# A 64-byte shift of the attention stage's tiles in SBUF

## The chip, the cores and the metric

The kernel runs on one core of one Trainium2 chip. The metric is device time of one execution in microseconds (us). The chip's engines go by short names: PE is TensorE (its matmuls; PEld are its weight loads, LDWEIGHTS), DVE is VectorE, ACT is ScalarE, POOL is GpSimd, and SP is SyncE, which issues all DMAs of this kernel. SBUF is the on-chip memory of 128 partitions; an "address" below is a byte offset inside a partition, the same in all of them.

## The reference

The input `x` is 2048 rows of 1024 float32 values. A conditioning vector gives six modulation rows (`mod`). The computation is one transformer-like block:

```python
h = _layernorm(x) * (1 + ca) + sa
x = x + ga * _A_ref(h, wq, wk, wv, wo, beta)     # attention with a memory
h = _layernorm(x) * (1 + cb) + sb
x = x + gb * _B_ref(h, w1, b1, w2, b2)           # MLP across the tokens
```

`_A_ref` projects `h` to queries, keys and values of 32 heads of 32 values, and cuts the 2048 rows into four segments of 512. In each segment a head does causal softmax attention, reads a memory matrix M with phi(q), mixes the two by a gate, and adds phi(k) v of the segment to M. The result goes through `wo`. `_B_ref` multiplies with a 2048 x 3584 matrix along the tokens, applies GELU, and multiplies back.

## The kernel before

Every large float32 product is done in three matmuls of `float32r` operands: each operand is split into a high part and a rest ("hi" and "lo"), and the products (hi, hi), (hi, lo), (lo, hi) are added in PSUM. So one operand tile of 512 columns is a `[128, 2, 512]` tile: 2048 bytes of hi, then 2048 bytes of lo.

The attention stage fills the first 1020 us. The normed input `h` lies in 16 "pages" of the pool `page` (`new_page`), one for each of 8 blocks of 128 channels and two segments at a time. The weights of one group of four heads lie in tiles `w` of the pool `paw` (tag `w`, 8 of them): `wv` holds keys and values, `wq` the queries. There are 32 iterations: two passes over pairs of segments, in each pass eight groups, in each group two segments. An iteration projects in two ways, and these two lines are where `w` and the pages meet on PE:

- `kv_chunk` (line 185, PSUM tile `nps`): the page is the stationary operand, 128 columns, and `w` the moving one, 256 columns. 96 matmuls an iteration, 3072 in all.
- `q_chunk` (line 193, PSUM tile `qps`): `w` is the stationary operand, 128 columns, and the page the moving one, 512 columns. 24 an iteration, 768 in all.

Each matmul has a weight load of its own, which runs beside the matmul ahead of it.

Between the projections of one iteration PE does the attention of others: `maxima` (line 421, `sx`, `sy`, `sz`) and `scores` (lines 443 to 450, `a`) read both operands out of one stacked tile `sk`; `values` (line 471, `pv`) multiplies the probabilities `ph` with `vp`; `memory` (lines 393 and 403, `rd` and `up`) reads and updates M (`MZ`); lines 353 and 486 transpose keys and results with the unit matrix `ident`. The order of the work is the order in which the main loop calls these pieces (`scores`, then `maxima` three heads ahead, then `values` one behind, then a piece of `project` eight ahead), as a planner that estimates times has interleaved them; the engines' queues keep that order. SP loads `w` tiles from DRAM for later groups (`load_w`), the second half of the modulation (`rawm`, line 497), stored input (`hre`), and copies `sg` into `sk` (`stack`).

After the attention come the output projection (`out_proj`, line 649, `po`: the pages hold `wo`, the stationary operand is `ots`) up to about 1253 us, and the MLP (`mix`, line 741, `mx`: the stationary operand is `sp`, the moving one `bA`, `bB` or `bU`) to the end. Both have the same three-product order and 512 moving columns as `q_chunk`.

SBUF is handed out in the order in which pools are opened. On the left side lie `const`, `page`, `par`, then `acst`, and above it the attention's other pools: `paw`, `st1`, later `prj`, `late` and `sk0`, `sk1`. On the right side lie `top` and, below it, `st2` and later `late2`. `acst` begins with a tile that nothing reads or writes, `pad2`. The output projection and the MLP close the attention's pools and place their own tiles from `page` upward and from the right end downward.

Of the kernel before, what the change touches and what calls it, by code (L numbers as in the profile page):

```python
# [7 lines left out]
F32 = mybir.dt.float32  # L8
# [10 lines left out]
P = 128  # L19
# [25 lines left out]
def attention_and_mlp(ctx, tc, x, wq, wkv, wo, beta, w1, b1, w2, b2, c, wm_a, wm_b, out):  # L45
# [22 lines left out]
    acst = acst_pool.__enter__()  # L68
    top_pool = tc.tile_pool(name="top", bufs=1, side="right")
    top = top_pool.__enter__()  # L70
    top.tile([P, 8], F32, name="pad")
    acst.tile([P, 8], F32, name="pad2")
    psum = ctx.enter_context(tc.tile_pool(name="psum", bufs=1, space=PSUM))

    def bank(tag, bufs, name):
# [868 lines left out]
```

## Time and profile before

| | us |
|---|---|
| median of 3 runs before | 2337.69 (2335.87 to 2338.27) |
| the profiled execution's own time | 2335.59 |
| its span, first to last instruction | 2333.9 |
| PE busy with matmuls | 2243.0 |
| PE busy with weight loads | 1925.1 |
| DVE busy | 1725.1 |
| ACT busy | 1102.0 |
| POOL busy | 678.4 |

The profiled execution is one run; its time is 2.10 us under the median of the three timed runs. A row of a group of instructions gives their line, engine, operation, the tiles (output, then inputs), the shapes, the count, the busy time in us and the mean duration of one in ns. The busy time is the time in which at least one of them ran: since matmuls are pipelined, the durations overlap, and 389 ns for one matmul doesn't mean that one starts each 389 ns. In a run of equal matmuls the time from one start to the next ("the step") is (length of the run - duration of the last) / (count - 1).

### The profile page before, as it was taken

To read this page: it belongs to the slowest core of one execution; us is meant where nothing else is said; L and a number is where in the kernel's file an instruction comes from. 1 tells how busy PE (TensorE), PEld (TensorE's weight loads), DVE (VectorE), ACT (ScalarE), POOL (GpSimd) and SP (SyncE) were. 2 spreads that over 40 slices of the span, in tenths; PEclk is the share of its full clock that TensorE was granted. 3 is DMA by queue.
4 is the path that set the end of the run, shared out by engine and by line. 5 is a ranking of instruction groups with operands and counts; after the bars stand their busy time and mean duration, and the time that the engine had idled before them with its cause. 6 is when DMAs were issued, how large, how long until landed. Compare 5 with 4: busy or idle time off the path is not lost.

```text
span 2333.9 us, 38273 instructions
## 1 busy us (share of the span) xinstructions
PE 2243.0 (96%) x13866; PEld 1925.1 (82%) x13866; DVE 1725.1 (74%) x3838; ACT 1102.0 (47%) x2002; POOL 678.4 (29%) x683
## 2 busy tenths in 40 slices
PE   8989999988889999998999999999999999999999
PEld 7888888877789999986877888888888788888887
DVE  6677777677766656657988656598889787868687
ACT  5476776645556666654334333353335242424232
POOL 3154544567755555545000000023332000000000
PEclk9999999999999999998999999999999999999999
DMA  6856666578844444473454765365557542423234
GB/s 244 250 153 178 179 186 184 166 231 260 259 131 115 129 119 119 106 229 129 149 195 166 295 228 198 140 252 213 214 213 272 185 136 72 145 66 129 68 112 150
DMA packets 164272, 406.27 MB, mean 174 GB/s; under 512 B 17108, under 2 KB 63220, under 8 KB 155124
## 3 DMA queue, kind: packets, MB, share of 16 engines
q1 hardware_dynamic: 164084, 403.83, 53.4%
q8 instruction: 110, 1.80, 0.3%
q14 instruction: 78, 0.64, 0.1%
HBM read 232.04 MB, written 120.86 MB: 151 GB/s over the span
## 4 chain that ended last, share of the span: by engine, by line
PE 80%; DVE 9%; DMA 6%; issue 2%; ACT 2%; SPq 1%; POOL 0%; DVEq 0%; ACTq 0%
PE mx L741 42%; PE nps L185 12%; PE qps L193 7%; PE po L649 6%; PE pv L471 3%; DMA rawm<-in_wm_b_dram 2%; PE sx L421 1%; PE a L443 1%; PE sz L421 1%; PE rd L393 1%; DVE bU L123 1%; PE up L403 1%; PE a L446 1%; PE a L450 1%; DVE sp L123 1%
## 5 line engine op out<-in xcount | busy, mean ns | idle before, releaser
L741 PE MATMUL mx<-bU,sp 128*128 128x512 f32 x2352 | 535.7, 389 | 3.7 <-DVE sp L123 2.3
L741 PEld LDWEIGHTS mx<-bU,sp 128*128 128x128 f32 x2352 | 440.8, 188 | 98.1 <-DVE sp L123 3.3
L185 PE MATMUL nps<-wv,h 128*128 128x256 f32 x3072 | 436.6, 284 | 1.4 <-DVE h L122 0.8
L741 PE MATMUL mx<-bA,sp 128*128 128x512 f32 x1764 | 433.4, 390 | 3.0 <-DVE sp L123 2.4
L120 ACT CAST sp<-wr 128x384 fp32r<-128x384 f32 (+2 forms) x408 | 217.2, 545 | 441.1 <-PE mx L741 369.3
L185 PEld LDWEIGHTS nps<-wv,h 128*128 128x128 f32 x3072 | 402.8, 191 | 6.9 <-DVE h L122 1.3
L741 PEld LDWEIGHTS mx<-bA,sp 128*128 128x128 f32 x1764 | 331.7, 188 | 73.6 <-DVE sp L123 2.9
L457 POOL TENSOR_TENSOR ph<-p,ph 128x1280 f16<-128x1280 f32 x128 | 344.6, 2693 | 146.7 <-ACT ph L456 146.5
L123 DVE TENSOR_TENSOR sp<-wr,sp 128x384 fp32r<-128x384 f32 (+2 forms) x408 | 260.7, 650 | 39.1 <-ACT sp L120 38.9
L748 DVE TENSOR_TENSOR ac<-mx,ac 128x512 f32<-128x512 f32 x280 | 189.2, 684 | 90.2 <-PE mx L741 89.3
L193 PE MATMUL qps<-h,wq 128*128 128x512 f32 x768 | 202.5, 411 | 3.7 <-DVE r L346 3.6
L649 PE MATMUL po<-wo,ots 128*128 128x512 f32 x768 | 183.8, 399 | 4.9 <-DVE x L652 2.0
L454 POOL TENSOR_SCALAR_AFFINE_SELECT p<-p 128x256 f32<-128x256 f32 x256 | 123.5, 489 | 192.5 <-ACT p L447 88.5
L649 PEld LDWEIGHTS po<-wo,ots 128*128 128x128 f32 x768 | 147.1, 193 | 37.3 <-ACT ots L120 3.3
L456 ACT CAST ph<-p 128x1280 f16<-128x1280 f32 x128 | 161.1, 1258 | 32.2 <-POOL p L454 31.8
L193 PEld LDWEIGHTS qps<-h,wq 128*128 128x128 f32 x768 | 147.2, 198 | 34.6 <-issue 3.7
L422 DVE CUSTOM_DVE_ANT_0 sx<-sx,mask 128x128 f32<-128x128 f32 (+1 forms) x256 | 110.1, 430 | 76.1 <-PE sx L421 74.8
L741 PE MATMUL mx<-bB,sp 128*128 128x512 f32 x588 | 164.9, 389 | 0.0
L471 PE MATMUL pv<-vp,ph 128*128 128x97 bf16 (+1 forms) x2560 | 148.7, 205 | 6.2 <-DVE red L478 4.2
L471 PEld LDWEIGHTS <-ph 128*128 128x128 f16 x2560 | 116.9, 100 | 30.2 <-issue 12.8
L748 DVE TENSOR_TENSOR cc<-mx,cc 128x512 f32<-128x512 f32 x140 | 94.6, 683 | 52.5 <-PE mx L741 48.9
L741 PEld LDWEIGHTS mx<-bB,sp 128*128 128x128 f32 x588 | 110.5, 188 | 23.0
(173 smaller groups left out, 3202.1 us busy)
## 6 DMA issues: line engine op xcount, KB each, us to landing
sk<-sg SPq DMA_DIRECT2D x384, 128.0 KB
wr<-in_w_dram SPq DMA_DIRECT2D x28, 1024.0 KB
wr<-in_w_dram SPq DMA_DIRECT2D x32, 768.0 KB
bstu<-ucd SPq DMA_DIRECT2D x28, 768.0 KB
wsp<-wv SPq DMA_DIRECT2D x32, 512.0 KB
rawm<-in_wm_b_dram SPq DMA_DIRECT2D x32, 512.0 KB
wv<-wsp SPq DMA_DIRECT2D x32, 512.0 KB
pcd<-cc SPq DMA_DIRECT2D x14, 1024.0 KB
```

Of the source, the lines that this page charges most:

```text
L120: A.copy(hi, src)
L123: lo_eng.tensor_tensor(lo, src, hi.bitcast(F32), op=ALU.subtract)
L185: T.matmul(ps[:, aa], h[:, j, 128 * tt:128 * tt + 128], wt[:, i, o:o + 256], start=(n == 0), stop=(n >= 6 * NK - 2), skip_group_check=True)
L193: T.matmul(ps, wt[:, i, o:o + 128], h[:, j], start=(k + n == 0), stop=(3 * k + n == 3 * NK - 1))
L422: V.tensor_tensor_reduce(o, o, mask[:, 384 - 128 * i:], 1.0, -3.0e38, op0=ALU.add, op1=ALU.max, accum_out=mx[:, h % 2, i:i + 1])
L454: G.affine_select(w, w, pattern=[[0, 2], [1, 128]], compare_op=ALU.is_ge, fill=0.0, base=0, channel_multiplier=-1)
L456: A.copy(ph[:, 0], p32)
L457: G.tensor_tensor(ph[:, 1], p32, ph[:, 0], op=ALU.subtract)
L471: T.matmul(pv[:, i, 0:w], ph[:, part, o:o + 128], d["vp"][:, j, h, 0:w], start=(n == 0), stop=(n == 19), skip_group_check=True)
L649: T.matmul(ps, os_[:, i, P * ct:P * ct + P], wop[ct, nh][:, j], start=(n == 0), stop=(n == 3 * NK - 1))
L741: T.matmul(ps, ops[q][:, i, P * k:P * k + P], b[:, j], start=(m == 0 and first), stop=(m == 3 * nk - 1), skip_group_check=True)
L748: V.tensor_tensor(d, ps, d, op=ALU.add)
```

## The change

A tile that nothing uses grows from 8 to 24 floats in each partition, 32 to 96 bytes. All that lies above it on the left side during the attention moves up by 64 bytes; nothing else in the text changes.

```diff
@@ -69,7 +69,7 @@
     top_pool = tc.tile_pool(name="top", bufs=1, side="right")
     top = top_pool.__enter__()
     top.tile([P, 8], F32, name="pad")
-    acst.tile([P, 8], F32, name="pad2")
+    acst.tile([P, 24], F32, name="pad2")
     psum = ctx.enter_context(tc.tile_pool(name="psum", bufs=1, space=PSUM))
```

The addresses before are those that the program as built gives its tiles; those after are 64 more for what lies above `pad2`. All modulo 256:

| tile | before | after |
|---|---|---|
| pages (`h`, later `wo`) | 224 | 224 |
| `w` (`wv`, `wq`) | 160 | 224 |
| `sk`, `sg` | 224 | 32 |
| `MZ`; `pq` | 160; 224 | 224; 32 |
| `v32`; `pk` | 160; 224 | 224; 32 |
| `vp` (three slots) | 224, 0, 32 | 32, 64, 96 |
| `ph`, `p32` | 32 | 32 |
| `k32`; `am`; `ident` | 160; 64; 64 | 224; 128; 64 |
| `ots`, `sp`, `bA`, `bB`, `bU` (output projection, MLP) | 224 | 224 |

Slices of `w` and of the pages begin at multiples of 512 bytes in their tiles, so that in lines 185 and 193 the two operands' starts differ by 64 modulo 256 before, and by 0 after. The tiles of the output projection and of the MLP don't move.

## The prediction

> **What bounds the kernel now.** I read the page's busy times and its chain first, then the chain and the busy times by stage, and last the durations of single matmul lines inside stages at full clock.
>
> ```profile
> span 2333.9 us, 38273 instructions
> PE 2243.0 (96%) x13866; PEld 1925.1 (82%) x13866; DVE 1725.1 (74%) x3838; ACT 1102.0 (47%) x2002; POOL 678.4 (29%) x683
> PE 80%; DVE 9%; DMA 6%; issue 2%; ACT 2%; SPq 1%; POOL 0%; DVEq 0%; ACTq 0%
> PE mx L741 42%; PE nps L185 12%; PE qps L193 7%; PE po L649 6%; PE pv L471 3%; DMA rawm<-in_wm_b_dram 2%; PE sx L421 1%; PE a L443 1%; PE sz L421 1%; PE rd L393 1%; DVE bU L123 1%; PE up L403 1%; PE a L446 1%; PE a L450 1%; DVE sp L123 1%
> ```
>
> PE is busy 96% of the span and holds 80% of the chain that ended last. The two lines whose operands the change brings together, nps and qps, hold 12% and 7% of it.
>
> The busy times by stage (columns: window, its length, busy us of PE, PEld, DVE, ACT, POOL with counts, granted clock, DMA share, GB/s):
>
> ```profile
> 100.00:700.00 600.00, 549.62 (x4582) 492.35 (x4581) 436.47 (x1212) 377.33 (x696) 330.42 (x314) 0.95 0.66 195
> 700.00:1000.00 300.00, 298.90 (x2714) 275.68 (x2710) 183.71 (x639) 188.44 (x333) 171.52 (x195) 1.00 0.46 120
> 1300.00:1500.00 200.00, 200.00 (x884) 165.62 (x883) 116.36 (x164) 64.85 (x115) 0.00 (x0) 1.00 0.55 204
> ```
>
> The attention has two halves. From 700 to 1000 us PE works 298.90 of 300 us at clock 1.00 and no other engine is busy for more than 188.44: what a matmul gets shorter there, the kernel gets shorter. From 100 to 700 us PE works 549.62 of 600 us at a mean clock of 0.95. The chain of each half says the same (first line of the view, from 100 to 700 us and from 700 to 1000 us; the view cuts it at its right end):
>
> ```profile
> by line: PE nps L185 20.5%; PE qps L193 13.4%; DMA rawm<-in_wm_b_dram 7.1%; PE pv L471 5.9%; issue 5.4%; PE sx L421 2.5%; PE a L443 2.3%; DMA hre<-hT 2.1%; PE up L403 2.1%; PE sz L421 2.0%; DVE sx L422 2.0%; DVE rawm L497 1.7%; PE a L446 1.
> ...
> by line: PE nps L185 39.2%; PE qps L193 20.1%; PE pv L471 11.2%; PE sz L421 3.8%; PE a L443 3.8%; PE sx L421 3.6%; PE rd L393 3.5%; DMA sk<-nt 3.0%; PE a L446 2.5%; PE a L450 2.5%; PE sy L421 2.0%; PE ops L486 1.7%; PE kps L353 1.6%; PE up
> ```
>
> **Does the distance of two operands cost time at all?** The same shape occurs with operands 64 apart modulo 256 (qps) and 0 apart (mx, po), all at full clock: durations as minimum/median/maximum, and the means of the groups, from 700 to 1000 us (nps, qps), 1300 to 1500 us (mx) and 1110 to 1174 us (po):
>
> ```profile
> L193 PE MATMUL qps<-h,wq x264: 387/392/483, 711.4 to 998.3; 128*128 128x512 f32 x132
> L185 PE MATMUL nps<-wv,h x1003: 275/276/368, 699.7 to 1000.0; 128*128 128x256 f32 x168
> L741 PE MATMUL mx<-bA,sp x664: 389/389/390, 1299.7 to 1499.9; 128*128 128x512 f32 x166
> ...
> L185 PE MATMUL nps<-wv,h 128*128 128x256 f32 x1003 | 141.9, 282 | 0.0
> L193 PE MATMUL qps<-h,wq 128*128 128x512 f32 x264 | 65.5, 397 | 0.0
> ...
> L649 PE MATMUL po<-wo,ots 128*128 128x512 f32 x284 | 64.6, 389 | 0.0
> ```
>
> In mx all 664 durations lie between 389 and 390 ns, and po has a mean of 389. The qps matmuls of the same shape have a median of 392 and a mean of 397. For nps the fastest are at 275, the median at 276, the mean at 282: half of them take longer than the floor. The timeline shows it as steps (start, length, count of a run of equal matmuls):
>
> ```profile
> 735.38 2.42 PE L185 MATMUL nps<-wv,h 128*128 128x256 f32 x19
> 767.81 4.52 PE L193 MATMUL qps<-h,wq 128*128 128x512 f32 x19
> 774.48 1.77 PE L185 MATMUL nps<-wv,h 128*128 128x256 f32 x14
> 791.36 2.48 PE L185 MATMUL nps<-wv,h 128*128 128x256 f32 x19
> 802.93 1.76 PE L185 MATMUL nps<-wv,h 128*128 128x256 f32 x14
> ...
> 1130.69 41.64 PE L649 MATMUL po<-wo,ots 128*128 128x512 f32 x183
> ```
>
> In po a step is (41.64 - 0.389) / 182 = 226.7 ns. In the qps run it is (4.52 - 0.392) / 18 = 229.3 ns. For nps, half the columns would take 226.7 / 2 = 113.3 ns; its four runs give (2.42 - 0.276) / 18 = 119.1, (1.77 - 0.276) / 13 = 114.9, 122.4 and 114.2 ns, 118.2 over the 62 steps together. So some runs are near the floor and some 6 to 9 ns over it, with the same distance of the operands in all.
>
> I take the distance as the likeliest cause of the excess inside runs: qps and mx have one shape and one order of products, DVE and ACT work beside both, and besides the stage I see no other difference. But part of the excess is the way into a run, when PE comes from other matmuls; that stays.
>
> The Trainium skill says the opposite of my reading: the page "TensorE: Matmul & The Clock Gate" (Part 2, step by step) gives PE two independent read ports of SBUF, so that loading the next weights takes no read bandwidth from the running matmul, and "SBUF — State Buffer" (section "SBUF: two separate sides") says that PE never waits on anyone. By these pages the sum below would be 0 us and the time the median before. The medians of 392 against 389 ns speak against them, though not about whose reads collide; the rival of no effect carries this reading.
>
> **The change part by part.**
>
> *The larger pad.* Nothing writes or reads it: no instruction, no DMA, no wait. Counting tile ends and starts from the addresses, no tile of the attention comes to overlap a later stage's tile that it didn't overlap before, so no new wait for a released tile; four overlaps with MLP buffers, loaded over 1000 us later, go away. Cost 0.
>
> *The pairing in qps.* 768 matmuls. The upper bound is the whole mean excess, 397 - 389 = 8 ns; the lower is 0 (a loss is a rival). I take the median's 392 - 389 = 3 ns, which the run above bears out (229.3 - 226.7 = 2.6), because the median leaves out the way into a run. That is 3/8 of the mean excess.
>
> *The pairing in nps.* 3072 matmuls. Upper bound 282 - 276 = 6 ns, lower 0. There is no row of 256 moving columns with operands 0 apart to take a value from, so I use the same fraction as in qps: 3/8 of 6 = 2.25 ns.
>
> *What of it reaches the end.* From 700 to 1000 us: 264 x 3 = 0.8 us and 1003 x 2.25 = 2.3 us, 3.1 us, all of it on PE's path. In the rest of the attention there are 768 - 264 = 504 qps and 3072 - 1003 = 2069 nps: 1.5 us and 4.7 us. How much of their time is on the chain I read from 100 to 700 us, by these groups:
>
> ```profile
> L185 PE MATMUL nps<-wv,h 128*128 128x256 f32 x1704 | 241.0, 283 | 0.9 <-DVE h L122 0.8
> L193 PE MATMUL qps<-h,wq 128*128 128x512 f32 x432 | 116.7, 421 | 3.6 <-DVE r L346 3.6
> ```
>
> 20.5% of 600 us is 123 us of chain for 241.0 us busy, 0.51; 13.4% is 80 us for 116.7, 0.69. So 4.7 x 0.51 + 1.5 x 0.69 = 2.4 + 1.0 = 3.4 us. What keeps the rest from counting is late already: the `rawm` loads (7.1% of that half's chain), which don't get faster. Sum of both pairings: 3.1 + 3.4 = 6.5 us. With the upper bounds it is 264 x 8 + 1003 x 6 = 8.1 us and 2069 x 6 x 0.51 + 504 x 8 x 0.69 = 9.1 us, 17.2 us; with the lower, 0.
>
> *Other matmuls whose operands move.* In the transposes of line 486 `am` and `ident` go from 0 apart to 64 apart; at most the same 3 ns on 128 of them, a loss of 0.4 us. In line 353 it goes from 96 to 160, and I have no reason for a sign. rd and up (lines 393, 403) keep their distance, and in sx, sy, sz and a both operands are in one `sk` tile. For pv the rows of `vp` are 194 bytes a head, so that its distances cover many values before and after; 0, and 1 us either way for the range.
>
> *DMAs.* All transfers keep their sizes, counts and order. Their rows in SBUF start off a multiple of 256 both before and after, `w` at 160 then 224, `sk` at 224 then 32. Only `sk<-nt` reaches the chain with 3.0% of 300 us, 9 us; a tenth of it either way is 0.9 us. I take 0.
>
> Together 6.5 - 0.4 = 6.1 us. The profiled execution's own time of 2335.59 becomes 2329.5, and the median of 2337.69, which is 2.10 us above it, becomes 2331.6. I say 2332.
>
> **The rivals.**
>
> *Both lines gain more: the way into a run is also part of it.* Then the upper bounds hold, up to 17 us: about 2321. Against it: the single sz and a matmuls, with both operands in one tile, also come out longer than 389 ns at full clock:
>
> ```profile
> L421 PE MATMUL sz<-sk 96*128 96x512 f32 x42 | 18.7, 446 | 0.0
> ```
>
> *Only qps gains.* Half of the nps durations are at 276 with the operands 64 apart, so that distance doesn't stop nps from running at its floor; its longer steps may have another cause. Then 0.8 + 1.0 = 1.8 us: 2335.9, no change that shows.
>
> *No effect.* The excess comes from the interleaving with other work and not from the operands' addresses; 2337.7. For it: the same nps medians. Against it: po comes with DVE and ACT work too and keeps 389.
>
> *Slower: nps takes the longer step for good.* In nps the weight load and the matmul are about equally long, unlike in po and mx, so equal starts may be the bad distance for it. If all its runs go at the pace of the two with 19 matmuls above, (2.144 + 2.204) / 36 = 120.8 ns instead of 118.2, it loses 2.6 ns on 1003 + 0.51 x 2069 = 2058 matmuls: 5.4 us, 2343. It decides the sign as soon as the nps step grows by 4.7 us / 2058 = 2.3 ns. For it: nps is the larger line and has two paces. Against it: mx and po show no second pace at distance 0.
>
> **How the numbers follow.** 0.2% is 4.7 us, about what a measurement of this kernel can tell from no change; faster is below 2333.0, slower above 2342.4. Chances: the forecast 0.45, with an own range of 2328 to 2335; more than that 0.05; only qps 0.18; no effect 0.16; slower 0.16. Faster: three quarters of the forecast's cases, 0.34, and the 0.05, and a remainder of 0.01 from qps alone: 0.40. Slower: most of the last, 0.13, and 0.02 from half-clock spells (clock 0.95 from 100 to 700 us) that fall otherwise: 0.15. The rest, 0.45, shows no change. The range of 2326 to 2343 leaves out about half of the 0.05, the deeper end of the forecast and part of the losses.
>
> **What would show it.** If right: 38273 instructions again; qps at a median of 389 and below 394 in the mean from 700 to 1000 us; a qps run of 19 in at most 4.48 us; the nps mean down from 282 to about 280, with fewer runs above 115 ns a step; the output projection starting some 6 us earlier; mx and po at 389 as before. If qps comes to 389 and nps keeps 282, it was qps alone. If both keep their rows, the address distance is no cause. If the nps mean goes above 284, it is the longer step. Wrong in another way would be rows of sx, a, pv or DMAs that change with their new addresses, or a first half in which gains on PE turn into longer waits for `rawm`.

## The result, and the profile after

The changed kernel takes 2341.99 us in the median of 22 runs (2334.26 to 2349.2), the kernel before 2337.53 us in 22 runs beside them (2332.69 to 2342.3). The ratio is 1.0021, with an interval of 1.0013 to 1.0028: the change costs 4.5 us, where 6.1 us of gain was forecast. The time lies close to the rival in which nps takes the longer step for good (2343).

The profiled execution after took 2343.58 us, 8.0 us more than that of before; so some 3.5 us of the difference between the two profiles is the spread from run to run. Part of that spread is the clock: from 100 to 700 us the granted clock was one half for 68.3 us in the profile after and for 61.4 us before (by the clock records of the two traces). At half clock a step of nps takes 214 ns (the median of 23 such steps before) instead of some 114, so by estimate the 6.9 us more are worth at most about half of that, 3.4 us. The medians don't differ by it: the mean granted clock is 0.979 over the 22 runs after, and 0.979 to 0.980 in each group of runs of the kernel before that was timed beside the experiments. The page of the changed kernel, its span, busy times and chain, and the groups of the two lines:

```profile
span 2341.9 us, 38273 instructions
PE 2252.5 (96%) x13866; PEld 1936.6 (83%) x13866; DVE 1736.0 (74%) x3838; ACT 1102.3 (47%) x2002; POOL 680.2 (29%) x683
PE 80%; DVE 9%; DMA 6%; issue 2%; ACT 2%; SPq 1%; POOL 1%; DVEq 0%; ACTq 0%
...
L185 PE MATMUL nps<-wv,h 128*128 128x256 f32 x3072 | 447.1, 288 | 3.8 <-DVE h L122 3.4
...
L193 PE MATMUL qps<-h,wq 128*128 128x512 f32 x768 | 202.7, 412 | 2.8 <-DVE r L346 2.6
```

The instructions are the same 38273, in the same order on every engine, and the shares of the chain are as before to within a point. PE is busy 9.5 us longer (2252.5 against 2243.0). The same two groups before:

```profile
L185 PE MATMUL nps<-wv,h 128*128 128x256 f32 x3072 | 436.6, 284 | 1.4 <-DVE h L122 0.8
...
L193 PE MATMUL qps<-h,wq 128*128 128x512 f32 x768 | 202.5, 411 | 3.7 <-DVE r L346 3.6
```

nps alone went up, by 10.5 us busy and 4 ns in the mean of one; qps stands still. The durations (minimum/median/maximum), group means, busy times by stage and the chain of the changed kernel, the stage from 700 to 1000 us at full clock first:

```profile
L185 PE MATMUL nps<-wv,h x1029: 276/283/367, 699.8 to 999.2; 128*128 128x256 f32 x172
L193 PE MATMUL qps<-h,wq x240: 387/389/481, 717.7 to 979.5; 128*128 128x512 f32 x120
...
L185 PE MATMUL nps<-wv,h 128*128 128x256 f32 x1029 | 149.3, 285 | 0.0
L193 PE MATMUL qps<-h,wq 128*128 128x512 f32 x240 | 59.2, 396 | 0.0
...
700.00:1000.00 300.00, 299.21 (x2708) 277.37 (x2706) 182.33 (x633) 188.26 (x331) 169.27 (x193) 1.00 0.43 118
100.00:700.00 600.00, 550.57 (x4538) 494.19 (x4537) 445.29 (x1200) 372.47 (x688) 326.78 (x310) 0.94 0.63 192
...
by line: PE nps L185 41.7%; PE qps L193 18.5%; PE pv L471 11.1%; PE a L443 3.8%; PE sz L421 3.8%; PE rd L393 3.6%; PE sx L421 3.6%; PE a L446 2.6%; PE a L450 2.5%; PE sy L421 2.0%; PE ops L486 1.7%; PE kps L353 1.5%; PE up L403 1.5%; PE a L
```

Now the median of nps is 283 ns instead of 276, and its mean 285 instead of 282. In qps the median fell from 392 to 389 ns, as the forecast had it, but the mean only from 397 to 396. From 100 to 700 us PE gets 4538 matmuls done instead of 4582, at a clock of 0.94 instead of 0.95. The runs of the timeline (start, length, count):

```profile
741.94 2.51 PE L185 MATMUL nps<-wv,h 128*128 128x256 f32 x19
753.39 1.83 PE L185 MATMUL nps<-wv,h 128*128 128x256 f32 x14
774.67 4.48 PE L193 MATMUL qps<-h,wq 128*128 128x512 f32 x19
...
1116.76 57.42 PE L649 MATMUL po<-wo,ots 128*128 128x512 f32 x252
```

The nps runs go at (2.51 - 0.283) / 18 = 123.7 and (1.83 - 0.283) / 13 = 119.0 ns a step, and none of those read goes at the 114 to 115 ns of the two runs of 14 before. The qps run goes at (4.48 - 0.389) / 18 = 227.3 instead of 229.3 ns, and po at 227.2 (226.7 in the run quoted before). Over all starts of single matmuls inside runs (a gap under 1.15 of 113.3 or 226.7 ns counts as inside) the mean step of nps rose from 115.7 to 119.4 ns, its quartiles from 113/114/118 to 118/120/120; that of qps fell from 230.2 to 228.8; po and mx stayed at 227.1 and 226.7.

Where the time lies, by the first and last po before (first row) and after (second row):

```profile
L649 PE MATMUL po<-wo,ots x768: 387/389/795, 1029.7 to 1251.4; 128*128 128x512 f32 x192
...
L649 PE MATMUL po<-wo,ots x768: 387/389/796, 1037.1 to 1259.0; 128*128 128x512 f32 x192
```

The output projection starts 7.4 us later and ends 7.6 us later, and the span is 8.0 us longer: 7.4 of the 8.0 us arise before it, in the attention.

### The profile page after: what moved, and what is told of

Same layout as the page of the kernel before. It is cut to its first block, busy times and chain, and to the rows that moved or that the text cites. A ratio compares the mean times of both kernels' runs of the same rounds, so it can differ in the third digit from the quotient of the medians.

```text
span 2341.9 us, 38273 instructions
## 1 busy us (share of the span) xinstructions
PE 2252.5 (96%) x13866; PEld 1936.6 (83%) x13866; DVE 1736.0 (74%) x3838; ACT 1102.3 (47%) x2002; POOL 680.2 (29%) x683
## 4 chain that ended last, share of the span: by engine, by line
PE 80%; DVE 9%; DMA 6%; issue 2%; ACT 2%; SPq 1%; POOL 1%; DVEq 0%; ACTq 0%
PE mx L741 43%; PE nps L185 12%; PE qps L193 7%; PE po L649 6%; PE pv L471 3%; DMA rawm<-in_wm_b_dram 2%; PE sx L421 1%; PE sz L421 1%; PE a L443 1%; DVE bU L123 1%; PE rd L393 1%; PE up L403 1%; PE a L446 1%; DMA bstu<-ucd 1%; DVE st L128 1%
## 5 line engine op out<-in xcount | busy, mean ns | idle before, releaser
L185 PE MATMUL nps<-wv,h 128*128 128x256 f32 x3072 | 447.1, 288 | 3.8 <-DVE h L122 3.4
L185 PEld LDWEIGHTS nps<-wv,h 128*128 128x128 f32 x3072 | 411.3, 193 | 9.1 <-DVE h L122 3.8
## 6 DMA issues: line engine op xcount, KB each, us to landing
sk<-sg SPq DMA_DIRECT2D x384, 128.0 KB
```

Of the source, the lines that this page charges most:

```text
L185: T.matmul(ps[:, aa], h[:, j, 128 * tt:128 * tt + 128], wt[:, i, o:o + 256], start=(n == 0), stop=(n >= 6 * NK - 2), skip_group_check=True)
```

## The experiments

My first theory after the result was that the step of a matmul depends on the distance between its stationary and its moving operand modulo 256, that 0 is good for 512 moving columns and bad for 256, and that nothing else in the change matters. The rivals were the other tiles that moved, DMA traffic, and work that runs beside the matmuls. "Distance" below is the start of `w` less that of the page, modulo 256: 192 before, 0 after.

### The distance by itself

This kernel does only the two kinds of runs, at ten distances, four runs at each, entered from another matmul of a different length each time; the block of the reference is left out. In its names `a` to `j` stand for 0, 32, 64, 96, 128, 160, 192, 224, 256 and 320; `kv` has the roles of nps and `q` those of qps.

```diff
+DIST = (0, 32, 64, 96, 128, 160, 192, 224, 256, 320)
...
+        t = pool.tile([P, 4 * 1024 + 128], F32R, tag="w", bufs=len(DIST), name=f"w{chr(97 + i)}")
+        V.tensor_copy(t[:, d // 4:d // 4 + 4096], raw)
...
+                                T.matmul(ps[:, o:o + 256], page[:, k, j, 128 * aa:128 * aa + 128],
+                                         w[:, k, a, 0:256], start=(n == 0), stop=(n >= 22), skip_group_check=True)
...
+                            T.matmul(ps, w[:, k, a, 0:128], page[:, k, j], start=(n == 0), stop=(n == 11))
```

> This kernel leaves out the whole computation: PE alone runs the operand streams of the two projection lines (kv: page stationary, 128 columns, w moving, 256; q: w stationary, page moving, 512), four runs of 24 or 12 matmuls for each of ten distances of w from the page (names a to j: 0, 32, 64, 96, 128, 160, 192, 224, 256, 320 bytes), with nothing else beside them. Theory of the distance: the step of kv depends on the distance, is about 119 ns at 0 (a), and 113.3 to 118 ns at 192 (g, the distance before); q is 226.7 ns at 0 and about 229 ns at 192; it repeats with 256, so that i is like a and j like c; some distance keeps kv at 113.3 throughout. Rival, two ports that never meet: all ten kv groups near 113.3 ns and all q groups near 226.7 ns, and the excess of the full kernel comes from the work beside it.

Its timeline (kv at 0, two neighbouring runs at 192; q at 0, 96, 192) and two pairs of groups:

```profile
35.85 3.04 PE L48 MATMUL kva<-wa,page 128*128 128x256 f32 x24
104.59 2.99 PE L48 MATMUL kvg<-wg,page 128*128 128x256 f32 x24
107.56 2.90 PE L48 MATMUL kvg<-wg,page 128*128 128x256 f32 x24
152.30 2.88 PE L52 MATMUL qa<-page,wa 128*128 128x512 f32 x12
190.39 2.97 PE L52 MATMUL qd<-page,wd 128*128 128x512 f32 x12
225.71 2.92 PE L52 MATMUL qg<-page,wg 128*128 128x512 f32 x12
...
L48 PE MATMUL kva<-wa,page 128*128 128x256 f32 x96 | 12.1, 284 | 0.0
L48 PE MATMUL kvg<-wg,page 128*128 128x256 f32 x96 | 11.8, 280 | 0.0
L52 PE MATMUL qa<-page,wa 128*128 128x512 f32 x48 | 11.5, 391 | 0.0
L52 PE MATMUL qi<-page,wi 128*128 128x512 f32 x48 | 11.6, 391 | 0.0
```

With 256 moving columns distance 0 takes (3.04 - 0.284) / 23 = 119.8 ns a step, and 192 has two paces, (2.99 - 0.280) / 23 = 117.8 and (2.90 - 0.280) / 23 = 113.9. With 512, 0 is the better of the two: (2.88 - 0.391) / 11 = 226.3 at 0, (2.92 - 0.395) / 11 = 229.5 at 192; and at 96 it is (2.97 - 0.397) / 11 = 233.9 (0.395 and 0.397 are the means of their groups). The steps in the second half of each run, worked out from the starts of single matmuls, where the way into the run is over (a comma between runs of one distance; where one value stands the runs lie within about 1 ns of it):

| distance | 0 | 32 | 64 | 96 | 128 | 160 | 192 | 224 | 256 | 320 |
|---|---|---|---|---|---|---|---|---|---|---|
| kv, ns | 120.0 | 116.7 | 117.8 | 120.0 | 118.4 to 120 | 117.1 to 118.6 | 113.3, 117.8, 113.3, 117.8 | 118.2 | 120.0 | 117.8 |
| q, ns | 226.7 | 233.3 | 233.3 | 234 | 230.8 to 232.8 | 233.3 | 228.8, 233.4, 228.4, 228.8 | 233.3 | 226.7 | 233.3 |

256 goes as 0 and 320 as 64, so the distance counts modulo 256. None of the ten keeps kv at 113.3 in all four runs, as was expected of one. No transfer of data and no other engine works beside these runs but for a copy of 8 columns at the end of each; about a dozen transfers of instructions are all that the DMA engines carry meanwhile. So the rival by which the excess comes from other work falls, and with it the prediction's "no effect". The rule quoted in the prediction from the Trainium skill ("TensorE: Matmul & The Clock Gate", Part 2, step by step), that a weight load takes no read bandwidth from the running matmul, would make all steps of a row equal; 113.3 to 120.0 ns here don't agree, though no run shows which unit is shared.

### The weights alone, and all but the weights

Two kernels split the change. The first moves only `w` by 64 bytes and all tiles after it by 256; the second moves everything that the change moves, but for `w`:

```diff
-    aw = paw.__enter__()
+    aw = paw.__enter__(); aw.tile([P, 16], F32, name="padw")
...
-    first_chunk(NK - 1)
+    first_chunk(NK - 1); aw.tile([P, 48], F32, name="padz")
```

> Only the w tiles move by 64 modulo 256 (to 224, like the pages); all other attention tiles keep their addresses modulo 256. Theory of the distance: as slow as the change itself, about 4 to 5 us over before (ratio 1.0015 to 1.0025), nps with a median duration of 283 ns from 700 to 1000 us and qps with 389. Rival, the other tiles that moved (sk, sg, vp, MZ, pq and so on): time of before (ratio 0.999 to 1.001), nps median 276 and qps 392.

```diff
-    acst.tile([P, 8], F32, name="pad2")
+    acst.tile([P, 24], F32, name="pad2")
...
-    aw = paw.__enter__()
+    aw = paw.__enter__(); aw.tile([P, 48], F32, name="padw")
...
-    first_chunk(NK - 1)
+    first_chunk(NK - 1); aw.tile([P, 16], F32, name="padz")
```

> All attention tiles above the pad but w move by 64 modulo 256; w stays at 160, 64 below the pages. Theory of the distance: time of before (ratio 0.999 to 1.001), nps median 276 ns and qps 392 ns from 700 to 1000 us. Rival, the other tiles: 4 to 5 us over before, with nps at 283.

Measured: 2342.02 against 2336.76 us for the weights alone (1.0025, interval 1.0015 to 1.0036), and 2335.57 against 2336.76 for all the others (0.9998, 0.9987 to 1.0009). The durations of both from 700 to 1000 us, the weights alone first:

```profile
L185 PE MATMUL nps<-wv,h x1017: 274/283/369, 699.8 to 997.5; 128*128 128x256 f32 x170
L193 PE MATMUL qps<-h,wq x241: 387/389/481, 716.1 to 999.8; 128*128 128x512 f32 x121
```

```profile
L185 PE MATMUL nps<-wv,h x996: 276/280/370, 699.8 to 991.1; 128*128 128x256 f32 x200
L193 PE MATMUL qps<-h,wq x264: 387/392/482, 711.7 to 999.2; 128*128 128x512 f32 x132
```

The first has the rows of the changed kernel, the second has the 392 ns in qps of before and a mean of 282 ns in nps (its median falls between the two paces). So the loss is the place of `w`, as far as the intervals go; `sk`, `vp`, `am`, `MZ` and the DMAs that end in them cost nothing that shows.

### A finer grid, a shorter weight load, and the roles exchanged

The same bare runs in steps of 8 bytes, and two more forms in steps of 32: `kh`, with 64 instead of 128 stationary columns, and `kq`, with `w` stationary and the page moving. The computation is left out as above. In the names `aa` is 0, `ba` 64, `bf` 104 and `bg` 112.

```diff
+    for form, dist in (("kv", FINE), ("q", FINE), ("kh", STEP), ("kq", STEP)):
...
+                                T.matmul(ps[0:64, o:o + 256], page[:, k, j, 128 * aa:128 * aa + 64],
+                                         w[:, k, a, 0:256], start=(n == 0), stop=(n >= 22), skip_group_check=True)
...
+                                T.matmul(ps[:, o:o + 256], w[:, k, a, 128 * aa:128 * aa + 128],
+                                         page[:, k, j, 0:256], start=(n == 0), stop=(n >= 22), skip_group_check=True)
```

> Again no part of the computation, PE alone with operand streams: kv and q at 32 distances of w from the page (0 to 248 in steps of 8; the first letter of a name counts 64 bytes, the second 8), and two further forms at 8 distances in steps of 32: kh (as kv, but 64 stationary columns, so that the weight load is half as long) and kq (as kv, but w stationary and the page moving). Theory that the two reads of PE meet: kv is the worst form because its weight load fills the whole step; with 64 columns kh keeps 113.3 ns at distance 0 while kv takes 120.0, and is no better than kv at distances where q also suffers; kq at distance d is like kv at 256 - d, so its best is at 64. Some distance between the steps of 32 may hold kv at 113.3 ns in all four runs. Rival, that a matmul of 256 columns costs the same whatever its weight load: kh is like kv, 120.0 ns at 0.

Its timeline:

```profile
35.69 3.04 PE L50 MATMUL kvaa<-w,page 128*128 128x256 f32 x24
189.56 3.23 PE L50 MATMUL kvbf<-w,page 128*128 128x256 f32 x24
204.68 2.88 PE L50 MATMUL kvbg<-w,page 128*128 128x256 f32 x24
796.55 2.90 PE L53 MATMUL khaa<-w,page 128*64 128x256 f32 x24
890.91 3.04 PE L56 MATMUL kqaa<-page,w 128*128 128x256 f32 x24
914.69 2.90 PE L56 MATMUL kqba<-page,w 128*128 128x256 f32 x24
```

Each bare kernel was executed once; kv at the distances that two of them share repeats to within 2 ns. By the same working over the second half of each run, kv keeps the floor of 113.3 ns at 112 alone (113.3, 113.3, 113.3, 114.5), and shows its two paces at 192 again. One run of four is at the floor at 16 too. Nearly all the others of the 32 distances go at 116.5 to 122, but at 8 and at 104 two runs of four take 126.6 and 130.7; the whole kvbf run above takes (3.23 - 0.286) / 23 = 128.0. q goes at 226.7 for 0 and 120, at 226.6 to 228.6 for 240, at 228.4 to 229.6 for 192, 229.2 for 176, and at 230 to 235 elsewhere. So the floor is the exception: most places cost 3 to 7% of a kv step, the worst run 15%, and most cost 1 to 3% of a q step.

With half the stationary columns (weight loads of 134 ns in the median instead of 192), `kh` at distance 0 goes at 113.3 ns in all four runs, where kv goes at 120.0. That fits a weight load that needs room inside the step, which 512 moving columns give and 256 don't: in the runs of the first bare kernel the weight loads of kv at 0 are busy 11.9 us beside 12.1 us of matmuls, those of q at 0 8.8 beside 11.5. But `kh` goes at 119.2 ns at distance 192, so room for the load doesn't heal every distance; and at 64, where q suffers, it goes at 113.3 in three runs of four, better than kv, which was not expected. That reading of why the two shapes differ is partly borne out and not shown. With the roles exchanged the good and the bad side exchange too: `kq` goes at 120.0 at 0 and 113.3 at 64, which is 192 seen from its stationary operand.

### Another bad distance in the full kernel

If the table of bare runs carries over, `w` at distance 96 is worse than 0, for there q is slow too:

```diff
-    aw = paw.__enter__()
+    aw = paw.__enter__(); aw.tile([P, 40], F32, name="padw")
...
-    first_chunk(NK - 1)
+    first_chunk(NK - 1); aw.tile([P, 24], F32, name="padz")
```

> Only the w tiles move, by 160, so that they lie 96 above the pages modulo 256, where the streams alone took 120.0 ns (kv) and 234 ns (q). Theory that the distance sets both lines: nps as in the change, with a median of 283 ns and a mean of 285 or more, and now qps longer too, with a median of 396 ns; the time 7 to 9 us over before, 2 to 4 over the change (ratio 1.003 to 1.004). Rival, that only equal addresses (distance 0) are special: qps and nps as before, ratio 0.999 to 1.001.

Measured: 2345.54 against 2337.93 us, 1.0031 (1.0017 to 1.0044), 7.6 us more. From 700 to 1000 us:

```profile
L185 PE MATMUL nps<-wv,h x1029: 274/281/368, 699.8 to 999.5; 128*128 128x256 f32 x172
L193 PE MATMUL qps<-h,wq x240: 390/397/482, 719.4 to 982.4; 128*128 128x512 f32 x120
```

Here qps has 390 as its minimum and 397 as its median, and its step inside runs is 233.8 ns; that of nps is 119.4, though its durations (281 in the median, 284 in the mean) lie a little under the 283 and 285 expected. The table of bare runs predicted the steps of the full kernel at a distance that no kernel had had. In the programs as built the page starts at 128 modulo 256 in the bare runs and at 224 in the full kernel, so it is the distance that carries over and not the address of either operand.

### Does the order of the products set the pace at 192?

At 192 kv has two paces, so a way to hold it at 113.3 would be a gain. I supposed that the order of (hi, hi), (hi, lo), (lo, hi) decides, and put three orders (`a`, `b`, `c`) and another order of loops (`kz`) into the bare runs, with eight ways in; the computation is left out again:

```diff
+ORDER = {"a": ((0, 0), (0, 1), (1, 0)), "b": ((0, 0), (1, 0), (0, 1)), "c": ((0, 1), (0, 0), (1, 0))}
...
+    for form in ("kva", "kvb", "kvc", "kza", "qa", "qb", "qc"):
```

> No part of the computation, PE alone: kv and q at eight distances (a to h: 0 to 224 in steps of 32) with three orders of the products (w part, page part): last letter before the distance a for (hi,hi),(hi,lo),(lo,hi) as in the kernel, b for (hi,hi),(lo,hi),(hi,lo), c for (hi,lo),(hi,hi),(lo,hi); kz is kv with the halves of the segment outside the products. Theory that the step hangs on the addresses of the weight load and of the matmul beside it, so also on which operand changes when: kvb at 192 (g) is what kq at 64 was in the run before, and holds 113.3 ns in all eight runs, where kva falls to 113.3 or 117.8 ns by the way into the run; at 0 every kv order takes 120.0 ns, and every q order 226.7 ns. Rival, the order plays no part: kvb and kvc like kva at each distance.

Durations at 192 in the order of the kernel and in the order `b`:

```profile
L52 PE MATMUL kvag<-w,page x192: 276/276/361, 172.8 to 196.0; 128*128 128x256 f32 x192
L52 PE MATMUL kvbg<-w,page x192: 276/276/361, 363.9 to 387.1; 128*128 128x256 f32 x192
```

They are alike, and so are the steps of all orders at every distance; at 192 each has runs of 113.3 and of 117.8 ns. This theory fell: among these orders only the distance and the way into the run count.

The same reordering in the full kernel:

```diff
-        for i, j in ((0, 0), (0, 1), (1, 0)):
+        for i, j in ((0, 0), (1, 0), (0, 1)):
```

> The kernel before, w at its old addresses, with the order of the three products in the kv projection changed to (hi,hi), (page hi, w lo)... that is (i,j) = (0,0), (1,0), (0,1); the same products are added in another order, and the planner interleaves somewhat otherwise. Theory: the nps step is held at 113.3 ns at distance 192, the nps median comes to 276 and the mean below 280 ns from 700 to 1000 us, and some 2 ns on about 2058 matmuls of the path are saved: 3 to 5 us under before (ratio 0.998 to 0.999). Rival, the order plays no part: nps mean 282 ns, ratio 0.999 to 1.001.

Measured: 2331.28 against 2337.09 us, 0.9971 (0.9954 to 0.9988). It is faster, but not by nps, whose row stands as it was (a mean of 282 ns again):

```profile
L185 PE MATMUL nps<-wv,h x1010: 276/277/367, 708.5 to 999.9; 128*128 128x256 f32 x169
L193 PE MATMUL qps<-h,wq x264: 387/392/483, 702.2 to 989.6; 128*128 128x512 f32 x132
...
L649 PE MATMUL po<-wo,ots x768: 387/389/775, 1020.0 to 1241.9; 128*128 128x512 f32 x192
...
100.00:700.00 600.00, 553.39 (x4661) 499.29 (x4660) 440.79 (x1224) 377.59 (x697) 343.76 (x322) 0.95 0.66 194
```

The planner interleaves the pieces in another way once the products are exchanged, and from 100 to 700 us PE gets 4661 matmuls done instead of 4582; po starts 9.7 us earlier. Which of the moved pieces does it was not isolated.

### Each projection at its own distance

Since kv wants 192 and q wants 0, the shared tag `w` was split into six buffers for `wv` and two for `wq`. The first kernel keeps both at 192; the second takes only `wv` to 0; the third takes only `wq` to 0:

```diff
-            w = aw.tile([P, 2, 512], F32R, tag="w", bufs=8, name=f"w{kind}{pr}_{g}_{part}_{i}")
+            w = aw.tile([P, 2, 512], F32R, tag=f"w{kind}", bufs=6 if kind == "v" else 2, name=f"w{kind}{pr}_{g}_{part}_{i}")
```

> A control for the two runs beside it: the eight shared buffers of w become six for wv and two for wq, all at the old distance (160, 64 below the pages); waits and order change a little with it. No theory says on which side of before it lies: ratio 0.996 to 1.004; nps mean 282 and qps mean 397 ns from 700 to 1000 us, as before.

```diff
-    aw = paw.__enter__()
+    aw = paw.__enter__(); aw.tile([P, 16], F32, name="padv")
...
+        if (kind, pr, g, part) == ("q", 0, 0, 0):
+            aw.tile([P, 48], F32, name="padq")
```

> As the control, with the same order of instructions, and only wv moved by 64 to the pages' 224. Theory that the loss is nps alone: 5 to 7 us over the control (a little more than the whole change costs), nps mean 285 ns or more, qps at 397 as in the control. Rival, nps and qps share the loss: 2 to 3 us over the control.

```diff
+        if (kind, pr, g, part) == ("q", 0, 0, 0):
+            aw.tile([P, 16], F32, name="padq")
...
-    first_chunk(NK - 1)
+    first_chunk(NK - 1); aw.tile([P, 48], F32, name="padz")
```

> As the control, and only wq moved by 64 to the pages' 224; wv stays 64 below. Theory: the part of the change that was right, taken alone; qps median 389 ns instead of 392 and 1 to 2 us under the control, nps as in the control. Rival, that moving wq costs too: 0 to 3 us over the control.

| kernel | us | ratio to before (interval) |
|---|---|---|
| split, both at 192 | 2313.78 | 0.9903 (0.9888 to 0.9917) |
| split, `wv` at 0 | 2320.33 | 0.9925 (0.9910 to 0.9941) |
| split, `wq` at 0 | 2316.02 | 0.9921 (0.9907 to 0.9935) |

The durations from 690 to 980 us, in the order of the table:

```profile
L185 PE MATMUL nps<-wv,h x960: 276/277/368, 702.9 to 974.7; 128*128 128x256 f32 x192
L193 PE MATMUL qps<-h,wq x252: 387/393/677, 694.8 to 979.9; 128*128 128x512 f32 x126
```

```profile
L185 PE MATMUL nps<-wv,h x976: 274/283/367, 689.8 to 978.7; 128*128 128x256 f32 x196
L193 PE MATMUL qps<-h,wq x240: 387/392/482, 696.7 to 959.2; 128*128 128x512 f32 x120
```

```profile
L185 PE MATMUL nps<-wv,h x960: 276/277/367, 699.7 to 971.2; 128*128 128x256 f32 x192
L193 PE MATMUL qps<-h,wq x262: 387/389/481, 691.9 to 979.1; 128*128 128x512 f32 x131
```

Each row answers to its own tile: 277 to 283 ns in nps with `wv` at 0, 393 to 389 in qps with `wq` at 0. In time, over 4, 6 and 6 runs, neither is clear. The first is a loss of 2320.33 - 2313.78 = 6.5 us by the medians, inside the 5 to 7 expected, but its interval still overlaps that of the control (0.9910 to 0.9917). The second should have been a gain of 1 to 2 us and came out 2.2 us longer, with a wider overlap; the qps gain is in the row, and whether it reaches the end stays open.

The split itself, with no distance changed, is the fastest kernel here, 21.6 us under the one before, far outside the 0.996 to 1.004 that was expected of a control. It changes which earlier tile each load of `w` has to see released, and with that the order in which the planner interleaves the work: PE, DVE, ACT and POOL all have another order of instructions than before, the same one in all three split kernels. Two rows of the waits from 20 to 1030 us, the kernel before first, then the split (us in all, times, longest):

```profile
SPq L434 <- ACT nt L429: 105.9, 31, 9.1
...
PE sx L421 <- DVE mx L422: 26.7, 20, 4.3
```

```profile
SPq L434 <- ACT nt L429: 47.1, 19, 6.7
...
PE sx L421 <- DVE mx L422: 10.5, 11, 2.4
```

SP waits 58.8 us less for `nt` at the copies of it into `sk`, and PE waits 16.2 us less at sx. But other waits grow: over all lines in that window SP waits 526.6 us before and 521.2 with the split, PE 55.6 and 44.6. So these rows go along with the gain and don't explain it; what in the new order makes it was not tried.

## Why the prediction was wrong

**That the distance costs time:** right, and shown by the bare runs. The rival of no effect falls with it, and those of qps alone and of a larger gain in both lines fall with the nps row.

**The pairing in qps:** right in the median (392 to 389 ns, and a run of 19 in 4.48 us, both as written), too large in size. The step inside runs fell by 1.4 ns in the kernel, not by 3, and the mean by 1 ns instead of at least 3. The difference of two medians of durations overstated the difference of the steps.

**The pairing in nps: the step that failed.** It reads "There is no row of 256 moving columns with operands 0 apart to take a value from, so I use the same fraction as in qps: 3/8 of 6 = 2.25 ns." The bounds beside it went from 0 to 6 ns of gain, with a loss left to a rival. The step went the other way, from 115.7 to 119.4 ns, 3.7 ns longer; the prediction's own sign of it, a mean of nps above 284 ns, came with 285. mx and po at 389 ns showed that 0 is good for 512 moving columns; they were taken as a witness for 256, for which 0 is one of the slower distances (120.0 ns in the bare runs).

**What reaches the end:** by the prediction's own count of matmuls on the path, 3.7 ns x 2058 = 7.6 us of loss less 1.4 ns x (264 + 0.69 x 504 = 612) = 0.9 us of gain, 6.8 us together. Measured are 4.5 us for the change and 5.3 us for the weights alone, so the path count gives half as much again as the one and over a quarter more than the other. The measured 2342 us lie inside the stated range of 2326 to 2343 only because that range reached up to the slower rival; the forecast itself had the wrong sign.

**The zero terms:** the pad, the other tiles and the DMAs are borne out by the kernel that moves all but `w` (0.9998).

**The slower rival:** right in its mechanism. It had the step at 120.8 ns from 118.2 in its quoted runs, +2.6 on 2058 matmuls, and 5.4 us. Its evidence was on view before: two paces of one line, and weight loads that are busy nearly as long as the matmuls in nps (402.8 us beside 436.6) and not in mx (440.8 beside 535.7):

```profile
L741 PEld LDWEIGHTS mx<-bU,sp 128*128 128x128 f32 x2352 | 440.8, 188 | 98.1 <-DVE sp L123 3.3
...
L185 PEld LDWEIGHTS nps<-wv,h 128*128 128x128 f32 x3072 | 402.8, 191 | 6.9 <-DVE h L122 1.3
```

That this is why equal starts are bad for nps is borne out in part by `kh` and not shown.

## What to carry to other kernels

Measure what a change to the placement does on the very shape that holds the path, here 256 moving columns: a row of another shape may have the other sign. Where a line already runs at its floor part of the time, as nps did at 192, ask how many places are better: of the other 31 distances tried only 112 had a shorter mean step, so a move was more likely to lose than to gain. Before tuning addresses, try which buffers share a tag: the kernel with one tag split is 21.6 us faster here, nearly three times what any address moved, though what in its new order of work makes the gain is open.

## What the runs showed of the hardware

- A `float32r` matmul's step depends on the distance of its two operands in SBUF, modulo 256 bytes: 113.3 to 122 ns for 256 moving columns in nearly all bare runs, and 126.6 and 130.7 in two runs each at the distances 8 and 104; 226.7 to 235 ns for 512. No other engine's work on the matrices ran beside them. The excess is mostly up to 8 ns a matmul in both shapes.
- The dependence isn't smooth. At 512 columns 0 and 120 hold the floor; at 256 only 112 does, and 192 does in some runs and not in others, by the way into the run, as do single runs at 16 and 64. Of the orders of the products that were tried none changes it.
- "SBUF — State Buffer" of the Trainium skill (section "SBUF: two separate sides") says that PE never waits on anyone. No other engine read SBUF beside the bare runs and the step at the ten distances still varied by 6%; if PE's reads don't wait on others, its own two operands disturb each other.
